# Where a float64 weight becomes two single-precision words: fewer steps on VectorE, and three GpSimd jobs moved to it

## The chip, the cores and the metric

The kernel runs on one core of a Trainium2 chip. Engines: TensorE (PE in the profile; PEld is its weight load), VectorE (DVE), ScalarE (ACT), GpSimd (POOL) and SyncE (SP), which only issues DMAs here. Each works through its own instruction list in order. The metric is the device time of one execution in microseconds (us).

## The reference

Three parts follow each other. All data are float32, except that `moe_w_in` and `moe_w_out` arrive as float64.

```python
# gated linear attention: q, k, v, f_logit are [4, 8, 768, 48]
f = 1 / (1 + exp(-f_logit))
for t in range(768):
    state = f[t] * state + outer(k[t], v[t]);  y[t] = q[t] @ state
x = y as [3072, 384]
# a dense FFN, w_in [384, 2048], w_out [2048, 384], both float64
h = x @ w_in
x = (max(h, 0) + log1p(exp(-|h|))) @ w_out
# a mixture of 8 experts on the tokens with x @ w_skip > 0
e = argmax(x @ w_gate);  p = softmax(x @ w_gate)[e]
out = x + p * (max(x @ w1[e], 0) @ w2[e])   # other tokens: out = x
```

## The kernel before

**Units and steps.** The FFN runs over 12 units of 256 tokens; each has 8 steps, one for each 256 columns of `w_in`. The main loop counts steps `s` from -20 to 95. A step of the FFN is `up` (matmuls of x with `w_in`), `act_a`, `act_b` and `act_c` (softplus) and `down` (matmuls with `w_out`). Every operand of these matmuls stands as two fp32r words, a rounded one (`hi`) and the remainder (`lo`), and three products are summed. Attention goes in 24 chunks of 128 tokens, in stages (`load`, `pre`, `decay`, `transpose`, `score`, `out`) that are laid some steps ahead of the unit that needs them. The experts follow behind unit 11.

**Conversion of the weights.** The float64 weights come in 8 groups (`load_w`): `si`, 256 columns of `w_in`, and `so`, 256 rows of `w_out`, 768 KB each, as pairs of 32-bit words. `conv_w(g, 0)` turns a group of `w_in` into `wi_hi`, `wi_lo`, and `conv_w(g, 1)` a group of `w_out` into `wo_hi`, `wo_lo`. The high word of a float64 holds its sign, an 11-bit exponent and 20 bits of the fraction; read as a float32 it is a float32 of another scale. The steps before: ScalarE takes the high word's absolute value (L218), VectorE clamps it from below (L220), masks and shifts it by 3 (L221), adds the two top bits of the high word (L222) and the top 3 bits of the low word (L223); ScalarE rounds the result to `hi` (L224), GpSimd subtracts to `lo` (L225). `tw` is the buffer that these steps share; there are two of it. For `so`, `route_cols` then multiplies the group with `w_skip` and `w_gate` on TensorE (L239 to L252). CONV_AT gives the step at which each group is converted: -8, -4, -1, 1, 2, 3, 4, 7. Groups 3 to 7 are so converted while unit 0 goes through its steps.

**Other work named below.** The gate's clamp (L273) is the first operation of `a_pre` on a chunk's `f_logit`, and waits for its DMA; the scans (L281, L282) of the same chunk read it, and free its buffer for the chunk two further on. For chunks 0 to 3 the clamp is VectorE's, from chunk 4 on GpSimd's (DVE_CHUNKS). In `act_c` the remainder `gl` (L442) is GpSimd's for the 8 steps of unit 0 (GL_POOL), and VectorE's from then on. GpSimd also has the addition of `act_b` (L433) and a mask for the first four chunks (L333).

**What sets the order.** The order in which the code issues instructions is only the start: a scheduler reorders each engine's list by a model of the times, except where the code pins it.

Of the kernel before, what the change touches and what calls it, by code (L numbers as in the profile page):

```python
# [40 lines left out]
def gla_softplus_moe_kernel(  # L41
# [156 lines left out]
    def load_w(g, parts=(0, 1)):
        n = 2 * P
        t = stage_t.setdefault(g, [None, None])  # L200
        if 0 in parts:
            t[0] = mw.tile([P, KD, 2 * n], I32, tag=f"w{2 * g % 4}", name=f"si{g}")
            sy.dma_start(out=t[0], in_=w_in32[:, g * 2 * n:(g + 1) * 2 * n].rearrange("(a p) c -> p a c", p=P))
        if 1 in parts:
            t[1] = mw.tile([P, 2, 2 * DM], I32, tag=f"w{2 * g % 4 + 1}", name=f"so{g}")
            sy.dma_start(out=t[1], in_=w_out32[g * n:(g + 1) * n, :].rearrange("(a p) c -> p a c", p=P))

    def conv_w(g, j):
        n = 2 * P
        src = stage_t[g][j].rearrange("p s (c two) -> p s c two", two=2)  # L210
# [5 lines left out]
        lo, hi = src[..., 0], src[..., 1]
        tf = t.bitcast(F32)
        se.activation(tf, hi.bitcast(F32), AF.Abs)  # L218

        (ge if 2 * g + j in MAX_POOL else ve).tensor_scalar(tf, tf, 2.0 ** -15, None, op0=ALU.max)  # L220
        ve.tensor_scalar(t, t, 0x07FFFFFF, 3, op0=ALU.bitwise_and, op1=ALU.logical_shift_left)  # L221
        ve.scalar_tensor_tensor(t, hi, -0x40000000, t, op0=ALU.bitwise_and, op1=ALU.bitwise_or)  # L222
# [952 lines left out]
```

## Time and profile before

| What | us |
|---|---|
| Median of 3 runs | 774.39 (773.63 to 779.21) |
| The profiled execution | 777.29 |
| Its span | 775.6 |
| TensorE busy (matmuls) | 703.9 |
| VectorE busy | 554.2 |
| ScalarE busy | 476.7 |
| GpSimd busy | 271.6 |

The span is the profiled execution's own, from its first to its last instruction. Busy time of an engine says little about a kernel of several stages: a table of stretches shows which engine is full in which stage, and the waits which engine the others wait for. A row's duration includes time in which the instruction could not get on.

### The profile page before, as it was taken

What the parts mean: (1) busy time and instruction counts of PE and PEld (TensorE: products, weight loads), DVE (VectorE), ACT (ScalarE), POOL (GpSimd) and SP (SyncE); (2) the same over time, 40 slices, a digit from 0 to 9 for tenths busy, and PEclk for the clock granted to TensorE, in tenths of its full rate; (3) what the DMA queues carried; (4) which work ended last, traced back from release to release, by engine and by line L of the source; (5) the groups of instructions that cost most, each with busy time, mean ns of one, the idle gap of its engine ahead of it and who ended that gap; (6) DMA issues with size and microseconds to landing.
All of it is one profiled execution on the core that took longest, in us unless ns stands there. A gap on an engine that the chain in (4) does not pass through costs nothing. (4 is left out here: it accounts for less than half of the span.)

```text
span 775.6 us, 15090 instructions
## 1 busy us (share of the span) xinstructions
PE 703.9 (91%) x5869; PEld 653.2 (84%) x5869; DVE 554.2 (71%) x1054; ACT 476.7 (61%) x863; POOL 271.6 (35%) x214
## 2 busy tenths in 40 slices
PE   2668788999999999999999999999989979999993
PEld 1557577898999999999999999999979878898883
DVE  8988997786767777767767786655866664865851
ACT  5647656566667667776666666755667643645750
POOL 4345775343343233423343232323322303321211
PEclk9869969799999999999999999999998999999997
DMA  9944421130213122211213122010423611655810
GB/s 293 258 149 129 128 83 43 53 95 25 72 53 95 53 75 69 59 54 48 89 53 96 53 63 62 14 46 8 159 67 121 252 42 51 209 204 179 292 74 11
DMA packets 36977, 77.19 MB, mean 100 GB/s; under 512 B 5967, under 2 KB 18594, under 8 KB 36896
## 3 DMA queue, kind: packets, MB, share of 16 engines
q1 hardware_dynamic: 34528, 71.89, 29.2%
q0 software_dynamic: 2368, 4.25, 1.9%
q8 instruction: 48, 0.79, 0.4%
q14 instruction: 33, 0.27, 0.1%
HBM read 64.89 MB, written 12.11 MB: 99 GB/s over the span
## 5 line engine op out<-in xcount | busy, mean ns | idle before, releaser
L406 PE MATMUL ph<-xh,wi 128*128 128x256 f32 x1152 | 235.6, 294 | 6.9 <-ACT wi L224 3.0
L433 POOL TENSOR_TENSOR w<-w,u 128x512 f32<-128x512 f32 x95 | 126.5, 1331 | 270.8 <-DVE u L426 182.0
L406 PEld LDWEIGHTS ph<-xh,wi 128*128 128x128 f32 x1152 | 193.1, 198 | 12.4 <-ACT wi L224 3.6
L406 PE MATMUL ph<-xl,wi 128*128 128x256 f32 x576 | 167.3, 290 | 0.6 <-DVE xl L383 0.6
L453 PE MATMUL acc<-wo_hi,gh 128*128 128x394 f32 x384 | 138.4, 362 | 3.0 <-ACT gh L441 2.4
L453 PE MATMUL acc<-wo_hi,gl 128*128 128x394 f32 x384 | 130.7, 348 | 3.8 <-DVE gl L442 3.4
L453 PE MATMUL acc<-wo_lo,gh 128*128 128x394 f32 x384 | 132.1, 344 | 0.0
L406 PEld LDWEIGHTS ph<-xl,wi 128*128 128x128 f32 x576 | 114.2, 198 | 1.3 <-DVE xl L383 0.9
L425 DVE SCALAR_TENSOR_TENSOR u<-w,u 128x512 f32<-128x512 f32 (+1 forms) x97 | 70.8, 731 | 37.2 <-ACT w L423 36.8
L442 DVE TENSOR_TENSOR gl<-w,gh 128x512 fp32r<-128x512 f32 (+1 forms) x89 | 60.9, 685 | 47.8 <-ACT gh L441 46.7
L421 ACT ACTIVATE u<-ph 128x512 f32<-128x512 f32 (+1 forms) x97 | 56.9, 587 | 49.8 <-PE ph L406 48.1
L432 ACT ACTIVATE w<-w 128x512 f32<-128x512 f32 (+1 forms) x97 | 60.7, 627 | 39.6 <-DVE u L425 39.5
L453 PEld LDWEIGHTS acc<-wo_hi,gh 128*128 128x128 f32 x384 | 72.8, 190 | 8.3 <-ACT gh L441 3.1
L441 ACT CAST gh<-w 128x512 fp32r<-128x512 f32 (+1 forms) x97 | 59.2, 611 | 30.8 <-POOL w L433 27.0
L453 PEld LDWEIGHTS acc<-wo_hi,gl 128*128 128x128 f32 x384 | 72.9, 190 | 5.9 <-DVE gl L442 4.5
L453 PEld LDWEIGHTS acc<-wo_lo,gh 128*128 128x128 f32 x384 | 73.6, 192 | 0.2 <-issue 0.2
L426 DVE SCALAR_TENSOR_TENSOR u<-ph,u 128x512 f32<-128x512 f32 (+1 forms) x97 | 65.8, 679 | 2.9
L651 DVE TENSOR_TENSOR w<-w,w 128x768 fp32r<-128x768 f32 x64 | 60.1, 984 | 8.1 <-ACT w L650 5.3
L423 ACT ACTIVATE w<-u 128x512 f32<-128x512 f32 (+1 forms) x97 | 60.6, 625 | 2.4 <-DVE gl L442 1.1
L422 ACT ACTIVATE u<-u 128x512 f32<-128x512 f32 (+1 forms) x97 | 60.7, 627 | 1.6
L766 PE MATMUL pom<-w,gh 128*128 128x384 f32 x208 | 55.8, 350 | 2.5 <-DVE om L776 2.5
L650 ACT CAST w<-w 128x768 fp32r<-128x768 f32 x64 | 49.7, 837 | 2.5 <-DMA w<-in_moe_w_dram 2.4
(197 smaller groups left out, 1233.3 us busy)
## 6 DMA issues: line engine op xcount, KB each, us to landing
w<-in_moe_w_dram SPq DMA_DIRECT2D x32, 768.0 KB
si<-in_moe_w_in_dram SPq DMA_DIRECT2D x8, 768.0 KB
so<-in_moe_w_out_dram SPq DMA_DIRECT2D x8, 768.0 KB
f<-in_f_logit_dram SPq DMA_DIRECT2D x24, 227.5 KB
q<-in_q_dram SPq DMA_DIRECT2D x24, 224.0 KB
k<-in_k_dram SPq DMA_DIRECT2D x24, 224.0 KB
x_s<-xr SPq DMA_DIRECT2D x24, 192.5 KB
v<-in_v_dram SPq DMA_DIRECT2D x24, 192.0 KB
```

The costliest lines, as they stand in the source:

```text
L406: te.matmul(ph[:, j, :], lhsT=w[i][:, kk, j * P:(j + 1) * P], rhs=x[:, kk, :], start=(n == 0), stop=(n == 3 * KD - 1))
L421: se.activation(u[:, c], ph[:, c], AF.Abs)
L422: se.activation(u[:, c], u[:, c], AF.Exp, scale=-1.0)
L423: se.activation(w[:, c], u[:, c], AF.Identity, bias=1.0)
L425: ve.scalar_tensor_tensor(u[:, c], w[:, c], 1.0, u[:, c], op0=ALU.subtract, op1=ALU.subtract)
L426: ve.scalar_tensor_tensor(u[:, c], ph[:, c], 0.0, u[:, c], op0=ALU.max, op1=ALU.subtract)
L432: se.activation(w[:, c], w[:, c], AF.Ln)
L433: (ve if i in self.fine else ge).tensor_tensor(w[:, c], w[:, c], u[:, c], op=ALU.add)
L441: se.copy(flat(gh)[:, c], w[:, c])
L442: (ge if i < self.pool_steps else ve).tensor_tensor(flat(gl)[:, c], w[:, c], flat(gh)[:, c].bitcast(F32), op=ALU.subtract)
L453: te.matmul(self.acc[t][:, 0:XR], lhsT=g[:, j, t * P:(t + 1) * P], rhs=w[f // 4][:, f % 4, :], start=(f == 0 and n == 0), stop=(f == NF - ...
L651: pin(ve.tensor_tensor(lo, t, hi.bitcast(F32), op=ALU.subtract))
```

## The change

ScalarE's pass takes the absolute value and scales it by 2**-112 at once, which puts the exponent where a float32 has it. The clamp (L220) is gone and the shift (L221) needs no mask; only the sign is taken from the high word. Three jobs of GpSimd go to VectorE: the weights' remainders (L225), the clamps of chunks 4 to 23 (L273), and unit 0's remainders `gl` (L442). The two weight tables are laid out anew before the launch, so that a group lies in one run of 6,144 bytes for each partition (before: three runs of 2,048 for `si`, two of 3,072 for `so`).

```diff
-DVE_CHUNKS = 4
-GL_POOL = 8
-MAX_POOL = ()
     def load_w(g, parts=(0, 1)):
...
+        for j in parts:
+            t[j] = mw.tile([P, 4 * DM], I32, tag=f"w{2 * g % 4 + j}", name=("si", "so")[j] + str(g))
+            sy.dma_start(out=t[j], in_=(w_in, w_out)[j][g].bitcast(I32))
     def conv_w(g, j):
...
-        se.activation(tf, hi.bitcast(F32), AF.Abs)
-        (ge if 2 * g + j in MAX_POOL else ve).tensor_scalar(tf, tf, 2.0 ** -15, None, op0=ALU.max)
-        ve.tensor_scalar(t, t, 0x07FFFFFF, 3, op0=ALU.bitwise_and, op1=ALU.logical_shift_left)
-        ve.scalar_tensor_tensor(t, hi, -0x40000000, t, op0=ALU.bitwise_and, op1=ALU.bitwise_or)
+        se.activation(tf, hi.bitcast(F32), AF.Abs, scale=2.0 ** -112)
+        ve.tensor_scalar(t, t, 3, None, op0=ALU.logical_shift_left)
+        ve.scalar_tensor_tensor(t, hi, -0x80000000, t, op0=ALU.bitwise_and, op1=ALU.bitwise_or)
         ve.scalar_tensor_tensor(t, lo, 29, t, op0=ALU.logical_shift_right, op1=ALU.bitwise_or)
-        se.copy(hw, tf)
-        ge.tensor_tensor(lw, tf, hw.bitcast(F32), op=ALU.subtract)
+        se.copy(hw, src)
+        ve.tensor_tensor(lw, src, hw.bitcast(F32), op=ALU.subtract)
     def a_pre(c):
-        (ge if c >= DVE_CHUNKS else ve).tensor_scalar(f, f, LOGIT_MIN, None, op0=ALU.max)
+        ve.tensor_scalar(f, f, LOGIT_MIN, None, op0=ALU.max)
     def act_c(self, i):
-                (ge if i < self.pool_steps else ve).tensor_tensor(flat(gl)[:, c], w[:, c], flat(gh)[:, c].bitcast(F32), op=ALU.subtract)
+                ve.tensor_tensor(flat(gl)[:, c], w[:, c], flat(gh)[:, c].bitcast(F32), op=ALU.subtract)
```

In the changed kernel's own line numbers L218 is L211, L221 to L225 are L212 to L216, L273 is L264, the scans L281 and L282 are L272 and L273, L300 is L291, L333 is L324, L433 is L423 and L442 is L432.

VectorE's list, from the first conversion step of group 0 on, before (`tw` is the conversion's buffer, `si` and `so` the loaded words, `qT`, `kT` and `f` attention's):

```order
L220 TENSOR_SCALAR tw<-tw 128x768
L221 TENSOR_SCALAR tw<-tw 128x768
L300 TENSOR_TENSOR qT_212<-q_130,eq_211 112x2x4x64
L222 SCALAR_TENSOR_TENSOR tw<-si_128,tw 128x768
L300 TENSOR_TENSOR kT_216<-k_132,ek_215 112x2x4x64
L223 SCALAR_TENSOR_TENSOR tw<-si_128,tw 128x768
L220 TENSOR_SCALAR tw<-tw 128x768
L273 TENSOR_SCALAR f_140<-f_140 112x520
L221 TENSOR_SCALAR tw<-tw 128x768
L222 SCALAR_TENSOR_TENSOR tw<-so_134,tw 128x768
L223 SCALAR_TENSOR_TENSOR tw<-so_134,tw 128x768
```

And now:

```order
L212 TENSOR_SCALAR tw<-tw 128x768
L213 SCALAR_TENSOR_TENSOR tw<-si_128,tw 128x768
L291 TENSOR_TENSOR qT_212<-q_130,eq_211 112x2x4x64
L291 TENSOR_TENSOR kT_216<-k_132,ek_215 112x2x4x64
L214 SCALAR_TENSOR_TENSOR tw<-si_128,tw 128x768
L212 TENSOR_SCALAR tw<-tw 128x768
L264 TENSOR_SCALAR f_140<-f_140 112x520
L213 SCALAR_TENSOR_TENSOR tw<-so_134,tw 128x768
L216 TENSOR_TENSOR wi_107<-tw,wi_107 128x768
L214 SCALAR_TENSOR_TENSOR tw<-so_134,tw 128x768
```

The two maxima (L220) are gone, and the first remainder (L216) stands between two steps of the next half's conversion.

GpSimd's list, behind its set-up, before:

```order
L225 TENSOR_TENSOR wi_107<-tw,wi_107 128x768
L333 AFFINE_SELECT a_sb<-a_sb 128x4x128
L225 TENSOR_TENSOR wo_lo_116<-tw,wo_hi_115 128x2x384
L333 AFFINE_SELECT a_sb<-a_sb 128x4x128
L225 TENSOR_TENSOR wi_108<-tw,wi_108 128x768
L225 TENSOR_TENSOR wo_lo_116<-tw,wo_hi_115 128x2x384
L273 TENSOR_SCALAR f_332<-f_332 112x520
L333 AFFINE_SELECT a_sb<-a_sb 128x4x128 x2
L273 TENSOR_SCALAR f_500<-f_500 112x520
L225 TENSOR_TENSOR wi_109<-tw,wi_109 128x768
L225 TENSOR_TENSOR wo_lo_118<-tw,wo_hi_117 128x2x384
```

And now:

```order
L324 AFFINE_SELECT a_sb<-a_sb 128x4x128 x6
L423 TENSOR_TENSOR w<-w,u 128x512 x3
L324 AFFINE_SELECT a_sb<-a_sb 128x4x128
L423 TENSOR_TENSOR w<-w,u 128x512
L324 AFFINE_SELECT a_sb<-a_sb 128x4x128
L423 TENSOR_TENSOR w<-w,u 128x512 x7
```

Of these only the masks (L333, now L324) and the additions (L433, now L423) stay on it.

VectorE's list from the scans of chunk 4 on (`f_332` before, `f_330` now), before:

```order
L281 SCALAR_TENSOR_TENSOR d_873<-restart,f_332 112x260
L282 SCALAR_TENSOR_TENSOR d_873<-restart,f_332 112x260
L252 TENSOR_TENSOR wo_lo_116<-pw_266,wo_hi_115 128x4x10
L222 SCALAR_TENSOR_TENSOR tw<-si_415,tw 128x768
L284 TENSOR_SCALAR hs_876<-d_873 112x4
L285 COPY hs_876<-d_873 112x4
L223 SCALAR_TENSOR_TENSOR tw<-si_415,tw 128x768
L315 TENSOR_TENSOR r_1035<-hs_587,hs_876 112x4
L286 TENSOR_TENSOR hmax<-hmax,hs_876 112x8
```

And now:

```order
L272 SCALAR_TENSOR_TENSOR d_862<-restart,f_330 112x260
L273 SCALAR_TENSOR_TENSOR d_862<-restart,f_330 112x260
L214 SCALAR_TENSOR_TENSOR tw<-si_411,tw 128x768
L216 TENSOR_TENSOR wo_lo_118<-tw,wo_hi_117 128x2x384
L309 TENSOR_TENSOR z_486<-ut,r_483 112x384
L243 TENSOR_TENSOR wo_lo_116<-pw_264,wo_hi_115 128x4x10
L275 TENSOR_SCALAR hs_865<-d_862 112x4
L276 COPY hs_865<-d_862 112x4
L216 TENSOR_TENSOR wi_110<-tw,wi_110 128x768
L264 TENSOR_SCALAR f_870<-f_870 112x520
```

Two remainders (L216) and the clamp of chunk 6 (L264, `f_870`) have come in; that clamp stands eight rows behind the scan which frees its buffer.

## Rows read from the trace of the kernel before

**Rows 1.** The profile's page: span and number of instructions.

```profile
span 775.6 us, 15090 instructions
```

**Rows 2.** Stretches: length, busy us of PE, PEld, DVE, ACT, POOL, PEclk, DMA, GB/s.

```profile
8.00:132.00 124.00, 91.00 (x765) 76.56 (x769) 112.63 (x155) 75.81 (x138) 70.64 (x42) 0.85 0.49 150
...
160.00:590.00 430.00, 424.75 (x3899) 401.93 (x3899) 302.91 (x651) 285.55 (x529) 147.77 (x114) 0.99 0.21 62
```

**Rows 3.** TensorE's waits, 8 to 132 us: us in total, times, longest.

```profile
PE pwt L239 <- DVE tw L223: 8.6, 4, 3.1
PE pw L244 <- DMA wsg<-in_moe_w_gate_dram: 4.5, 1, 4.5
```

**Rows 4.** VectorE's groups, 8 to 132 us: busy us, mean ns, idle before.

```profile
L221 DVE TENSOR_SCALAR tw<-tw 128x768 int32<-128x768 int32 x16 | 15.0, 938 | 0.2
L222 DVE SCALAR_TENSOR_TENSOR tw<-so,tw 128x768 int32<-128x768 int32 x8 | 11.6, 1448 | 0.1
L220 DVE TENSOR_SCALAR tw<-tw 128x768 f32<-128x768 f32 x16 | 11.6, 722 | 6.5 <-ACT tw L218 6.5
L222 DVE SCALAR_TENSOR_TENSOR tw<-si,tw 128x768 int32<-128x768 int32 x8 | 9.9, 1241 | 0.0
...
L284 DVE TENSOR_SCALAR hs<-d 112x4 f32<-112x4 f32 x6 | 5.5, 913 | 0.0
```

**Rows 5.** Instructions on the tile tw: shortest, median, longest in ns.

```profile
L220 DVE TENSOR_SCALAR tw<-tw x16: 528/553/1671, 8.0 to 127.3; 128x768 f32<-128x768 f32 x16
L221 DVE TENSOR_SCALAR tw<-tw x16: 546/556/3539, 8.5 to 128.0; 128x768 int32<-128x768 int32 x16
...
L224 ACT CAST wi<-tw x8: 817/832/835, 12.1 to 121.8; 128x768 fp32r<-128x768 f32 x8
```

**Rows 6.** The timeline, at 7 and around 42 us: start, duration, instruction.

```profile
7.21 0.14 DVE L284 TENSOR_SCALAR hs<-d 112x4 f32<-112x4 f32 x1
...
41.63 2.14 POOL L273 TENSOR_SCALAR f<-f 112x520 f32<-112x520 f32 x1
...
42.44 3.54 DVE L221 TENSOR_SCALAR tw<-tw 128x768 int32<-128x768 int32 x1
...
43.74 1.82 POOL L225 TENSOR_TENSOR wi<-tw,wi 128x768 fp32r<-128x768 f32 x1
```

**Rows 7.** Prices on VectorE: shortest, median, longest of three lines, whole run.

```profile
L651 DVE TENSOR_TENSOR w<-w,w x64: 945/952/2231, 574.4 to 749.9; 128x768 fp32r<-128x768 f32 x64
...
L442 DVE TENSOR_TENSOR gl<-w,gh x89: 418/685/873, 156.6 to 633.1; 128x512 fp32r<-128x512 f32 x87, 128x256 fp32r<-128x256 f32 x2
...
L273 DVE TENSOR_SCALAR f<-f x4: 422/426/851, 3.7 to 30.7; 112x520 f32<-112x520 f32 x4
```

**Rows 8.** GpSimd's groups, 8 to 132 us.

```profile
L225 POOL TENSOR_TENSOR wi<-tw,wi 128x768 fp32r<-128x768 f32 x8 | 15.8, 1977 | 17.3 <-ACT wi L224 17.3
L225 POOL TENSOR_TENSOR wo_lo<-tw,wo_hi 128x768 fp32r<-128x768 f32 x7 | 15.8, 2257 | 15.3 <-ACT wo_hi L224 15.3
L442 POOL TENSOR_TENSOR gl<-w,gh 128x512 fp32r<-128x512 f32 x7 | 12.6, 1799 | 3.0 <-ACT gh L441 3.0
L433 POOL TENSOR_TENSOR w<-w,u 128x512 f32<-128x512 f32 x7 | 9.9, 1409 | 7.2 <-DVE u L426 6.4 <-ACT w L432 0.8
L273 POOL TENSOR_SCALAR f<-f 112x520 f32<-112x520 f32 x5 | 9.5, 1907 | 6.8 <-DMA f<-in_f_logit_dram 6.8
L333 POOL TENSOR_SCALAR_AFFINE_SELECT a_sb<-a_sb 128x512 f32<-128x512 f32 x8 | 7.7, 983 | 3.1 <-ACT a_sb L332 3.0
```

**Rows 9.** The timeline: a gate's load and its clamp; a held-up conversion step.

```profile
54.30 0.33 SPq L263 DMA_DIRECT2D f<-in_f_logit_dram  x1
...
57.16 1.50 POOL L273 TENSOR_SCALAR f<-f 112x520 f32<-112x520 f32 x1 [5.59 <-DMA f<-in_f_logit_dram]
...
126.37 0.92 ACT L218 ACTIVATE tw<-so 128x768 f32<-128x768 f32 x1 [1.16 <-POOL wi L225]
...
127.32 0.67 DVE L220 TENSOR_SCALAR tw<-tw 128x768 f32<-128x768 f32 x1 [4.96 <-ACT tw L218]
```

More of the change, by code (lines that the diff above doesn't have):

```diff
@@ L47, in gla_softplus_moe_kernel @@
     f_logit: bass.AP,
-    w_in64: bass.AP,
-    w_out64: bass.AP,
+    w_in: bass.AP,
+    w_out: bass.AP,
     w_skip: bass.AP,
@@ L62, in gla_softplus_moe_kernel @@
     B = NT // S
-    DFF = w_in64.shape[1]
+    DFF = w_in.shape[0] * 2 * P
     E = w1.shape[0]
@@ L191, in clear_routes @@
         sy.dma_start(out=table.rearrange("(p c) o -> p (c o)", p=P), in_=t[:, 0:E * KT])
-    w_in32 = w_in64.bitcast(I32)
-    w_out32 = w_out64.bitcast(I32)
     stage_t = {}
     def load_w(g, parts=(0, 1)):
-        n = 2 * P
         t = stage_t.setdefault(g, [None, None])
[L201 to L206, printed above, removed]
+        for j in parts:
+            t[j] = mw.tile([P, 4 * DM], I32, tag=f"w{2 * g % 4 + j}", name=("si", "so")[j] + str(g))
+            sy.dma_start(out=t[j], in_=(w_in, w_out)[j][g].bitcast(I32))
@@ L208, in conv_w @@
     def conv_w(g, j):
-        n = 2 * P
-        src = stage_t[g][j].rearrange("p s (c two) -> p s c two", two=2)
-        t = att.tile([P, 2 * DM], I32, tag="tw", name="tw", bufs=2).rearrange("p (a c) -> p a c", a=src.shape[1])
+        lo, hi = (stage_t[g][j][:, n::2] for n in range(2))
+        t = att.tile([P, 2 * DM], I32, tag="tw", name="tw", bufs=2)
+        tf = t.bitcast(F32)
         if j == 0:
-            hw, lw = wi_hi[g], wi_lo[g]
+            hw, lw = (w[g].rearrange("p a c -> p (a c)") for w in (wi_hi, wi_lo))
+            src = tf
@@ L214, in conv_w @@
         else:
             hw, lw = (w[g // 2][:, g % 2 * 2:g % 2 * 2 + 2, 0:DM] for w in (wo_hi, wo_lo))
[L216 to L222 removed]
+            src = tf.rearrange("p (a c) -> p a c", a=2)
@@ L226, in conv_w @@
         if j == 1:
-            route_cols(g, tf)
+            route_cols(g, src)
     wt_ps = {}
@@ L391, in gla_softplus_moe_kernel, with __init__ @@
     class Ffn:
-        def __init__(self, x, fine=(), pool_steps=0):
+        def __init__(self, x, fine=()):
             self.x = x
             self.fine = fine
-            self.pool_steps = pool_steps
             self.h, self.w, self.cc, self.g = {}, {}, {}, {}
@@ L870, in gla_softplus_moe_kernel @@
                 if i == 0:
-                    ffns[u] = Ffn(xhl[u], FINE if u == NU - 1 else (), GL_POOL if u == 0 else 0)
+                    ffns[u] = Ffn(xhl[u], FINE if u == NU - 1 else ())
                 ffns[u].up(i)
@@ L1146, in _layout @@
         r = a.reshape(4, 2, -1, a.shape[1])
-        return _np.concatenate([r[:, :, :32].reshape(-1, a.shape[1]),
-                                r[:, :, 32:].transpose(0, 2, 1, 3).reshape(-1, a.shape[1])], 0)
+        r = _np.concatenate([r[:, :, :32].reshape(-1, a.shape[1]),
+                             r[:, :, 32:].transpose(0, 2, 1, 3).reshape(-1, a.shape[1])], 0)
+        return r.reshape(-1, P, a.shape[1] // 256, 256).transpose(2, 1, 0, 3).reshape(-1, P, 2 * r.shape[0])
+    if name == "moe_w_out":
+        return a.reshape(-1, 2, P, a.shape[1]).transpose(0, 2, 1, 3).reshape(-1, P, 2 * a.shape[1])
     return a
```

## The prediction

> **What bounds the kernel now.** I began with the span and the table of stretches [rows 1, 2]. From 160 to 590 us TensorE is busy for 424.75 of 430 us: nothing that VectorE (DVE), ScalarE (ACT) or GpSimd (POOL) saves there can shorten the run. The stretch to look at is 8 to 132 us, in which the eight groups of FFN weights are converted: VectorE is busy for 112.63 of 124 us, TensorE for 91.00, ScalarE for 75.81, GpSimd for 70.64 [rows 2]. TensorE's waits there end on VectorE's last conversion step (L223) for 8.6 us, and once on a DMA for 4.5 us [rows 3]. So VectorE sets the pace of this stretch, and 33 us of TensorE's idle time can be won at most.
>
> Next I looked at how VectorE spends its 112.63 us. Its rows are longer than their work. L221 averages 938 ns, with a median of 556; 16 of them are 15.0 - 16 x 0.556 = 6.1 us too long. L220 in the same way: 11.6 - 16 x 0.553 = 2.8. L222 against 0.952, the median of another two-input operation of its shape: 11.6 + 9.9 - 16 x 0.952 = 6.3 [rows 4, 5, 7]. L284 works on 4 columns; six of them take 5.5 us, where an undisturbed one takes 0.14: 4.7 [rows 4, 6]. The same reckoning for L223, L425, L281, L282, L300, L288, L315 and L318, each against its shortest row in the first 150 us, gives 13.1. Together 33 us. Where it comes from shows in one place: the L221 that starts at 42.44 us takes 3.54 us, and beside it GpSimd runs a gate clamp and then a remainder until 45.56 [rows 6]; VectorE ends 0.42 us after that. Of the 41 VectorE rows before 145 us that are stretched by over 0.1 us, all overlap a GpSimd instruction. So VectorE pays for work that stands on GpSimd's list.
>
> **The change part by part.** All of it falls into the same stretch, but for 15 later clamps.
>
> The max on VectorE (L220) goes: 16 x 0.553 = -8.8 us [rows 5]. The step after it keeps its shape and loses one of two operations; a one-operation L220 and a two-operation L221 on the same shape take 0.553 and 0.556 [rows 5], so that is nothing. ScalarE's pass keeps its count and shape: a scale in it costs nothing that I can price, and ScalarE has 48 us free here [rows 2].
>
> The remainders of the split (L225) go to VectorE: 16 instructions. The same shape, types and operation stands on VectorE at L651 with a median of 952 ns [rows 7]: +15.2. Unit 0's eight remainders (L442), of which GpSimd ran seven in this stretch [rows 8]: 7 x 0.685 [rows 7] = +4.8. The clamps (L273), five here [rows 8]: 5 x 0.424 (four of them ran on VectorE, shortest 422 ns [rows 7]) = +2.1. Work on VectorE: -8.8 + 15.2 + 4.8 + 2.1 = +13.3.
>
> Against that the stretching. GpSimd's time here is 15.8 + 15.8 + 12.6 + 9.5 = 53.7 us in what moves away, and 9.9 + 7.7 = 17.6 in what stays (L433, L333) [rows 8]. Shared out by time, 75% of the 33 us go: -24.8. The bounds: at best all 33 go; at worst what stays stretches a denser VectorE by all of its 17.6 us in place of 8.2, and only 33 - 17.6 = 15.4 go. I take the share, since the pairs of rows give about the same (L225 alone some 15.6 us of the stretch).
>
> The Trainium skill (SBUF — State Buffer, section "Who interferes with whom") says that VectorE and GpSimd share one pair of ports, and that who comes first holds it for the whole instruction while the other is blocked; that agrees with the 3.54 us row. By this rule alone, with every microsecond of the moved work blocking, 53.7 us would go and the run would gain some 40 us; the measured stretch of 33 us in all refuses that.
>
> A hold-up goes too. At 127.32 us VectorE had been idle for 4.96 us for ScalarE's next pass, and that pass had waited for GpSimd to finish a remainder, since it writes the buffer the remainder reads [rows 9]; before that the GpSimd queue held up an addition as well. With remainders of 0.95 us in place of about 2 us [rows 7, 8], I take 4 of the 4.96: -4.0 (bounds 0 and -4.96).
>
> New waits. VectorE takes its list in order, so each moved instruction can now stop it. (a) A remainder needs ScalarE's cast, 0.832 us [rows 5]. In the new order the work between a group's L223 and its remainder is 1.4 us at the least and mostly 2 to 4, so 0. (b) A clamp needs its gate's DMA, which is issued only when the scan two chunks earlier has freed the buffer. At 54.30 us that load is issued and at 57.16 the clamp starts, 2.9 us later, after 5.59 us of GpSimd's idling [rows 9]. The new order puts 3.0 to 4.2 us of other VectorE work between scan and clamp for chunks 5 to 8, so a prompt load is hidden; SyncE's queue is in order too, and may not be prompt. Bounds 0 and 5.6 each; I take 0.7 each for five, the nearer row being the 2.9 against 3.0: +3.5. (c) Up to 30 us the load engines are full, and TensorE waits 4.5 us for the small gate weights [rows 3]; a faster VectorE then reaches work that TensorE has not finished. Bounds 0 and 6; I take +3.0.
>
> The weight tables are laid out anew, so that each of a partition's loads is one run of 6 KB in place of three of 2 or two of 3. No row prices that; the bytes stay, and I take nothing, with 1 us either way. From 160 to 590 us VectorE has 127 us free [rows 2], which covers 15 clamps of 0.42 us and the last remainder of unit 0.
>
> Sum for VectorE's stretch: +13.3 - 24.8 - 4.0 + 3.5 + 3.0 = -9.0 us. TensorE follows it, since its idle time here (33 us) is well above that. The profiled execution took 777.29 us (span 775.6 us [rows 1] and 1.7 us around it); it would take 768.3. It lies 2.9 above the median of 774.39, so the forecast is **765.4 us**, 1.2% below. With the bounds above, the gain is between 0 and about 18: the forecast's own range is 757 to 772.
>
> **The rivals.**
>
> *TensorE is the next bound.* It is busy for 91.00 of the 124 us [rows 2]. If half of VectorE's saving lands where TensorE is full, the gain is 4.5 us: 770. Against it: the waits on VectorE's steps stand at the top of its list [rows 3].
>
> *The clock gives more.* The granted clock was 0.85 in 8 to 132 us and 0.99 in 160 to 590 [rows 2]: in the stretch with the gaps TensorE is at the lower of its two levels (1.2 in place of 2.4 GHz) for some three tenths of the time. At full clock the same work would have taken about 91.00 x 0.15 = 14 us less. If a denser TensorE wins 8 of these where it is itself the bound, the time is 757. It is as likely that the lower level just falls elsewhere, so I leave this out of the sum.
>
> *VectorE stands behind late gates (slower).* If each of the five clamps waits as GpSimd's did at 57.16, 5.6 us [rows 9], that is 28 us in place of 3.5: -9.0 + 24.5 = +15.5, so 790. It decides from 2.5 us a clamp: there the gain is gone. The order speaks against it (3.0 us of cover at the least), the single SyncE queue for it.
>
> *VectorE only gets more work (slower).* If the stretch is VectorE's own and stays, +13.3 - 4.0 + 6.5 = +15.8: 790. The overlap of all 41 stretched rows with GpSimd speaks against it. The Trainium skill (Perfetto Trace Analysis, section "Optimizing Scalar/DVE Operations") says that a saturated VectorE may give work to GpSimd, which this change undoes; it adds at once that between these two that may not help.
>
> **How the numbers follow.** The forecast gets 0.52, TensorE as the bound 0.26, the clock 0.11, late gates 0.07, more work 0.04. A difference of 1%, 7.7 us, is about what a measurement of this kernel tells from no change (its three runs spread over 5.6 us); faster by over 1% means under 766.6. Of the forecast's 0.52 some 0.43 lie below that, with all of the clock's 0.11: 0.54 faster. The rest of the forecast and all of the second case give 0.35 within 1%. The two slower ones give 0.11. The range has to reach the second case and the clock's: 756 to 776; left out are the two slower cases and the tails.
>
> **What would show it.** In 8 to about 122 us of the changed profile: no max; 16 remainders on VectorE of about 0.95 us; GpSimd busy for under 20 us; the last conversion step near 122 us in place of 132; L221's mean near 0.6 us, and L284's near 0.2. TensorE busy without a gap from then on. Wrong would be: VectorE rows still stretched where GpSimd is idle (the stretch was VectorE's own); VectorE idle for more than 12 us in the stretch, ended by the gate's DMA or by ScalarE's casts (the new waits were too small); the last conversion step at 122 us but the run no shorter, with the time back as TensorE's idle time behind 132 us or as a lower granted clock.

## The result, and the profile after

The changed kernel takes 754.84 us (median of four runs, 753.31 to 757.98), the kernel before beside it 775.92 us (773.63 to 779.21). The ratio is 0.973, with a 95% interval of 0.968 to 0.978: 21 us or 2.7% faster. I had forecast 765.4 us, 9 us below before, with a range that began at 756.

The profiled execution of the changed kernel took 757.98 us, its longest, against 777.29 us for the one of before. From its page: the span, and each engine's busy time with its share and instructions.

```profile
span 756.3 us, 15057 instructions
...
PE 695.6 (92%) x5869; PEld 644.7 (85%) x5869; DVE 539.2 (71%) x1082; ACT 476.1 (63%) x863; POOL 198.5 (26%) x170
```

VectorE's and GpSimd's busy times have both fallen, by 15 and 73 us; ScalarE's has stayed (against the table of the time before). Where they fell, the table of stretches shows (length, busy us of PE, PEld, DVE, ACT, POOL, then PEclk, DMA share, GB/s). The last conversion step now ends at 112.54 us in place of 132.16, so the first row here answers to the 8 to 132 us of before [rows 2].

```profile
8.00:114.00 106.00, 84.57 (x792) 70.31 (x794) 98.76 (x168) 75.82 (x138) 23.77 (x15) 0.94 0.54 175
...
160.00:590.00 430.00, 424.84 (x3863) 402.69 (x3862) 299.10 (x652) 283.42 (x523) 125.56 (x99) 0.99 0.23 70
```

In 106 us VectorE is busy for 98.76 (93%), GpSimd for 23.77 where it had 70.64, and TensorE for 84.57 at a granted clock of 0.94 (before: 0.85). From 160 to 590 us nothing has changed, as one expects of a stretch that TensorE fills. VectorE's groups in 8 to 114 us (busy us, mean ns, idle before):

```profile
L212 DVE TENSOR_SCALAR tw<-tw 128x768 int32<-128x768 int32 x16 | 9.8, 610 | 2.3 <-ACT tw L211 2.3
L213 DVE SCALAR_TENSOR_TENSOR tw<-so,tw 128x768 int32<-128x768 int32 x8 | 8.7, 1090 | 0.1
L216 DVE TENSOR_TENSOR wo_lo<-tw,wo_hi 128x768 fp32r<-128x768 f32 x8 | 8.5, 1068 | 0.4 <-ACT wo_hi L215 0.3
L213 DVE SCALAR_TENSOR_TENSOR tw<-si,tw 128x768 int32<-128x768 int32 x8 | 7.6, 951 | 0.0
L216 DVE TENSOR_TENSOR wi<-tw,wi 128x768 fp32r<-128x768 f32 x8 | 7.6, 950 | 0.0
...
L432 DVE TENSOR_TENSOR gl<-w,gh 128x512 fp32r<-128x512 f32 x7 | 4.8, 682 | 2.4 <-ACT gh L431 2.4
...
L264 DVE TENSOR_SCALAR f<-f 112x520 f32<-112x520 f32 x8 | 3.8, 470 | 1.8 <-DMA f<-in_f_logit_dram 1.8
...
L275 DVE TENSOR_SCALAR hs<-d 112x4 f32<-112x4 f32 x6 | 2.5, 410 | 0.0
```

Line by line against [rows 4]: the max is gone, the shift (L212, was L221) takes 610 ns in place of 938, the step after it 951 and 1090 in place of 1241 and 1448, the four columns of L275 410 in place of 913. The 16 remainders (L216) have come in at 950 and 1068 ns. VectorE's waits there (us in total, times, longest):

```profile
DVE gl L432 <- ACT gh L431: 2.4, 1, 2.4
DVE tw L212 <- ACT tw L211: 2.3, 5, 0.6
DVE f L264 <- DMA f<-in_f_logit_dram: 1.8, 1, 1.8
```

And TensorE's:

```profile
PE pk L299 <- DVE kT L291: 10.9, 1, 10.9
...
PE pw L235 <- DMA wsg<-in_moe_w_gate_dram: 4.5, 1, 4.5
...
PE pwt L230 <- DVE tw L214: 1.5, 2, 1.2
```

TensorE waits for the last conversion step for 1.5 us, where it was 8.6 [rows 3]; the wait for the small gate weights is the same 4.5. The first line is the start-up, TensorE's wait for the first `kT`; before it was 11.3 us, the longest of TensorE's waits there, which [rows 3] doesn't show. Its last 3 us come after the 8 us mark, so they are among the 33 us of idle time that the prediction counted as there to be won. What is left on GpSimd in the same stretch:

```profile
L423 POOL TENSOR_TENSOR w<-w,u 128x512 f32<-128x512 f32 x7 | 12.7, 1814 | 31.5 <-DVE u L416 20.1 <-ACT w L422 6.3 <-ACT w L413 5.2
L324 POOL TENSOR_SCALAR_AFFINE_SELECT a_sb<-a_sb 128x512 f32<-128x512 f32 x8 | 11.2, 1403 | 47.6 <-ACT a_sb L323 47.6
```

Both groups have grown longer, the addition from 1409 to 1814 ns and the mask from 983 to 1403 [rows 8]. TensorE's wait for a mask is 1.6 us (before: 2.3), so that costs little. That the denser VectorE does it is not shown: in e6 below VectorE is as full (94% of the stretch), and the mask takes 922 ns.

The end of FFN unit 0 shows that the whole gain arises here: the timeline's copy of its first result (start, duration, instruction) in the kernel before,

```profile
155.74 0.49 ACT L473 COPY xr<-acc 128x394 f32<-128x394 f32 x1 [0.50 <-PE acc L453]
```

and in the changed one:

```profile
133.32 0.47 ACT L463 COPY xr<-acc 128x394 f32<-128x394 f32 x1
```

That is 22.4 us earlier. The eleven units behind it end 40 to 48 us apart in both kernels and give back 3 us in all; the span is 19.3 us shorter.

**One account for every kernel.** I take the stretch from VectorE's first conversion step (7.96 us) to the end of the last one, and split its length in three: *idle* is the sum of the waits that the timeline gives behind VectorE's rows; *stretching* is the sum over its rows of what each takes beyond the shortest row of its line and shape in the first 150 us; *work* is the rest. In us, of the profiled executions, one for each kernel; GpSimd's busy time and the granted clock are those of the stretch, and "unit 0" is the start of the copy above.

| kernel | time, median | ratio to before, 95% | stretch | work | stretching | idle | GpSimd busy | clock | unit 0 |
|---|---|---|---|---|---|---|---|---|---|
| before | 775.92 | | 124.2 | 79.5 | 34.0 | 10.7 | 70.6 | 0.85 | 155.7 |
| changed | 754.84 | 0.9730 (0.9679 to 0.9782) | 104.6 | 90.1 | 8.0 | 6.5 | 23.8 | 0.93 | 133.3 |
| e1_moves | 762.28 | 0.9803 (0.9761 to 0.9845) | 111.0 | 97.1 | 8.7 | 5.2 | 25.0 | 0.95 | 138.6 |
| e2_nomax | 768.86 | 0.9894 (0.9859 to 0.9929) | 120.3 | 72.0 | 28.2 | 20.1 | 72.8 | 0.86 | 150.1 |
| e3_layout | 774.12 | 0.9974 (0.9945 to 1.0003) | 127.7 | 79.5 | 34.5 | 13.7 | 70.8 | 0.91 | 158.5 |
| e4_ghost | 764.64 | 0.9848 (0.9806 to 0.9889) | 115.4 | 88.7 | 16.9 | 9.8 | 83.9 | 0.87 | 143.8 |
| e5_rest_back | 760.59 | 0.9795 (0.9766 to 0.9824) | 110.2 | 84.1 | 15.1 | 11.1 | 41.5 | 0.83 | 139.9 |
| e6_split_back | 764.26 | 0.9841 (0.9816 to 0.9866) | 111.8 | 77.1 | 29.3 | 5.4 | 49.7 | 0.85 | 143.2 |
| e7_masks | 748.65 | 0.9651 (0.9630 to 0.9671) | 105.1 | 94.6 | 7.3 | 3.2 | 12.1 | 0.97 | 130.7 |
| e8_hold | 765.67 | 0.9878 (0.9850 to 0.9905) | 120.2 | 90.8 | 23.9 | 5.5 | 90.3 | 0.86 | 146.8 |
| e9_adds | 748.83 | 0.9648 (0.9601 to 0.9695) | 97.1 | 92.7 | 3.5 | 0.9 | 10.5 | 0.93 | 128.9 |
| e10_masks_adds | 754.59 | 0.9726 (0.9677 to 0.9774) | 101.2 | 96.7 | 1.7 | 2.8 | 0.0 | 0.93 | 135.1 |
| e11_masks_only | 766.37 | 0.9887 (0.9859 to 0.9916) | 118.3 | 84.5 | 28.3 | 5.6 | 67.7 | 0.88 | 142.4 |
| e12_warm | 754.80 | 0.9723 (0.9684 to 0.9761) | 102.6 | 89.7 | 8.4 | 4.6 | 25.7 | 0.98 | 132.3 |

So the change made VectorE's stretch 19.6 us shorter: +10.6 of work, -26.0 of stretching, -4.2 of idling.

### The profile page after: what moved, and what is told of

Same layout as the page of the kernel before. It is cut to its first block, busy times and chain, and to the rows that moved or that the text cites. A ratio compares the mean times of both kernels' runs of the same rounds, so it can differ in the third digit from the quotient of the medians.

```text
span 756.3 us, 15057 instructions
## 1 busy us (share of the span) xinstructions
PE 695.6 (92%) x5869; PEld 644.7 (85%) x5869; DVE 539.2 (71%) x1082; ACT 476.1 (63%) x863; POOL 198.5 (26%) x170
## 5 line engine op out<-in xcount | busy, mean ns | idle before, releaser
L396 PE MATMUL ph<-xh,wi 128*128 128x256 f32 x1152 | 230.8, 289 | 2.0 <-DVE wi L216 1.0
L423 POOL TENSOR_TENSOR w<-w,u 128x512 f32<-128x512 f32 x95 | 128.7, 1355 | 339.2 <-DVE u L416 213.4
L396 PEld LDWEIGHTS ph<-xh,wi 128*128 128x128 f32 x1152 | 188.9, 194 | 7.0 <-issue 2.4
L396 PE MATMUL ph<-xl,wi 128*128 128x256 f32 x576 | 164.5, 286 | 0.0
L396 PEld LDWEIGHTS ph<-xl,wi 128*128 128x128 f32 x576 | 111.9, 194 | 0.0
L432 DVE TENSOR_TENSOR gl<-w,gh 128x512 fp32r<-128x512 f32 (+1 forms) x97 | 65.9, 681 | 46.2 <-ACT gh L431 45.5
L415 DVE SCALAR_TENSOR_TENSOR u<-w,u 128x512 f32<-128x512 f32 (+1 forms) x97 | 67.8, 699 | 34.1 <-ACT w L413 33.8
L411 ACT ACTIVATE u<-ph 128x512 f32<-128x512 f32 (+1 forms) x97 | 57.2, 589 | 51.6 <-PE ph L396 49.8
```

The costliest lines, as they stand in the source:

```text
L396: te.matmul(ph[:, j, :], lhsT=w[i][:, kk, j * P:(j + 1) * P], rhs=x[:, kk, :], start=(n == 0), stop=(n == 3 * KD - 1))
L411: se.activation(u[:, c], ph[:, c], AF.Abs)
L415: ve.scalar_tensor_tensor(u[:, c], w[:, c], 1.0, u[:, c], op0=ALU.subtract, op1=ALU.subtract)
L423: (ve if i in self.fine else ge).tensor_tensor(w[:, c], w[:, c], u[:, c], op=ALU.add)
L432: ve.tensor_tensor(flat(gl)[:, c], w[:, c], flat(gh)[:, c].bitcast(F32), op=ALU.subtract)
```

## Experiments

My theory: VectorE sets the pace of the conversion; its rows are stretched by what GpSimd does beside them, and work that leaves GpSimd takes the stretching along. The rivals: the gain comes from the max alone, or from the new layout of the weights; TensorE's clock gives it; GpSimd's remainders cost by holding the buffer `tw`, and not by slowing VectorE's rows.

### The three parts of the change, each alone

**e1_moves**: before, with the three moved jobs on VectorE; max, masks and layout stay.

```diff
-DVE_CHUNKS = 4
+DVE_CHUNKS = 24
-GL_POOL = 8
+GL_POOL = 0
-        ge.tensor_tensor(lw, tf, hw.bitcast(F32), op=ALU.subtract)
+        ve.tensor_tensor(lw, tf, hw.bitcast(F32), op=ALU.subtract)
```

> The kernel before with only the three jobs moved to VectorE: the max, the mask and the old layout stay. My theory (VectorE is stretched by GpSimd's work, and sets the pace of the stretch): +22 us of work, -25 us of stretching and -4 us of hold-up, so 4 to 13 us faster than before, with GpSimd busy under 25 us up to the last conversion step and VectorE's L284 near its undisturbed 0.14 us. Rival 1 (the removed max alone makes the gain, a job costs the same on either engine): within 3 us of before, or slower. Rival 2 (the stretching is VectorE's own): 15 us or more slower.

Measured: 762.28 us against 776.86 of before beside it, -14.6 us. Stretching falls from 34.0 to 8.7 us, work grows by 17.6, idling halves. The 14.6 us are 1.6 more than the expectation's range allowed. By the prediction's own terms the moves were worth next to nothing: -24.8 + 15.2 + 4.8 + 2.1 - 4.0 + 6.5 = -0.2 us. Here lies the whole miss. The account puts the stretch at -13.2 us, 13.0 from that sum: the waits came 8.0 us lower (-5.5 for +2.5), the work 4.5 lower (17.6 for 22.1) and the stretching 0.5.

**e2_nomax**: before, with the new arithmetic alone.

```diff
-        se.activation(tf, hi.bitcast(F32), AF.Abs)
-        (ge if 2 * g + j in MAX_POOL else ve).tensor_scalar(tf, tf, 2.0 ** -15, None, op0=ALU.max)
-        ve.tensor_scalar(t, t, 0x07FFFFFF, 3, op0=ALU.bitwise_and, op1=ALU.logical_shift_left)
-        ve.scalar_tensor_tensor(t, hi, -0x40000000, t, op0=ALU.bitwise_and, op1=ALU.bitwise_or)
+        se.activation(tf, hi.bitcast(F32), AF.Abs, scale=2.0 ** -112)
+        ve.tensor_scalar(t, t, 3, None, op0=ALU.logical_shift_left)
+        ve.scalar_tensor_tensor(t, hi, -0x80000000, t, op0=ALU.bitwise_and, op1=ALU.bitwise_or)
```

> The kernel before with only the new arithmetic: scale in ScalarE's pass, no max, no mask; the three jobs stay on GpSimd, the old layout stays. My theory: VectorE saves 16 x 0.55 = 8.8 us and is stretched as before, so 7 to 12 us faster. Rival 1 (the max alone makes the gain): 18 to 22 us faster. A third reading, that the collisions just move to other rows and take the saving back: within 3 us of before.

Measured: 768.86 against 776.86, -8.0 us, close to the -8.8 that the prediction gave the max. The account shows that it is not that simple: work and stretching fall by 13.3 us together, and 9.4 come back as idling. VectorE's waits in 8 to 128 us:

```profile
DVE tw L220 <- ACT tw L218: 13.2, 5, 6.4
```

ScalarE's pass writes a buffer that GpSimd's remainder reads, so the hold-up of [rows 9] is the first suspect; e8 below puts it to the test. In the longest wait, the 6.4 us up to 123.85, ScalarE's list stood behind GpSimd three times: 1.60 us for a clamp, 0.97 for an addition and 1.15 for the buffer.

**e3_layout**: before, with the new layout of the weights alone (in the changed kernel the old arithmetic, and the three jobs on GpSimd again).

```diff
-        se.activation(tf, hi.bitcast(F32), AF.Abs, scale=2.0 ** -112)
-        ve.tensor_scalar(t, t, 3, None, op0=ALU.logical_shift_left)
+        se.activation(tf, hi.bitcast(F32), AF.Abs)
+        ve.tensor_scalar(tf, tf, 2.0 ** -15, None, op0=ALU.max)
+        ve.tensor_scalar(t, t, 0x07FFFFFF, 3, op0=ALU.bitwise_and, op1=ALU.logical_shift_left)
...
-        ve.tensor_tensor(lw, src, hw.bitcast(F32), op=ALU.subtract)
+        ge.tensor_tensor(lw, src, hw.bitcast(F32), op=ALU.subtract)
```

> The kernel before with only the new layout of the two weight tables, one run of 6144 bytes a partition. My theory: within 3 us of before. Rival 3 (fuller loads in the first 30 us start everything sooner): 5 us or more faster, with TensorE's wait for the small gate weights shorter than 4.5 us.

Measured: 774.12 against 776.86; the interval of the ratio, 0.9945 to 1.0003, holds 1. The layout is worth nothing that this measurement can tell. The parts add up: -14.6 and -8.0 make -22.6, the change gave -21.1. In the profiled executions the stretch is 13.2 and 3.9 us shorter and 3.5 us longer than before in e1, e2 and e3, and their times lie at -14.4, -4.4 and +1.6; the first two make 17.1 of the 19.6 us by which the change shortens it, so there the sum holds only roughly. Neither the max alone nor the layout carries the gain.

### Does GpSimd's reading alone slow VectorE?

**e4_ghost**: the changed kernel, with four reads by GpSimd beside each conversion; they touch no buffer that VectorE waits for, and their result is not used.

```diff
         ve.tensor_tensor(lw, src, hw.bitcast(F32), op=ALU.subtract)
+        gt = att.tile([P, P + 64], F32, tag="gt", name="gt", bufs=1)
+        for n in range(4):
+            part = hw[:, n * 192:(n + 1) * 192] if j == 0 else hw[:, n // 2, n % 2 * 192:(n % 2 + 1) * 192]
+            ge.tensor_tensor(gt, part.bitcast(F32), part.bitcast(F32), op=ALU.subtract)
```

> The changed kernel, in which GpSimd also reads each new hi word again and writes a difference that nobody uses: 64 instructions of 128x192, no buffer of the conversion is held by them. My theory: GpSimd's reads alone stretch VectorE again, 10 to 18 us slower than the changed kernel, VectorE's rows longer where they overlap L220 on GpSimd. Rival 2 (the stretching is VectorE's own, GpSimd's time is free): within 3 us of the changed kernel. They also stand ahead of the masks and additions in GpSimd's list, which may add a few us in either theory.

Measured: 764.64 us, some 9.8 above the changed kernel (ratios 0.985 and 0.973), where 10 to 18 were expected. Stretching goes from 8.0 to 16.9. GpSimd's added groups in 8 to 123 us:

```profile
L220 POOL TENSOR_TENSOR gt<-wi 128x192 f32<-128x192 f32 x32 | 36.7, 1147 | 12.6 <-ACT wi L215 10.6
L220 POOL TENSOR_TENSOR gt<-wo_hi 128x192 f32<-128x192 f32 x28 | 23.3, 831 | 13.6 <-ACT wo_hi L215 12.1
```

So work on GpSimd that nobody waits for lengthens VectorE's rows, at a low price: 60 us of these reads add 8.9 us of stretching. The run's 9.8 us are not that alone. The reads stand in GpSimd's list ahead of masks and additions; TensorE waits 8.1 us for late masks (changed kernel: 1.6), and VectorE once 4.1 us for TensorE:

```profile
PE py L350 <- POOL a_sb L328: 8.1, 3, 5.3
```

In e8, next, the masks are hardly late, and the stretching stands by itself.

**e8_hold**: e4 with one of the two inputs taken from the buffer `tw`, so that GpSimd holds it as the old remainder did.

```diff
-            ge.tensor_tensor(gt, part.bitcast(F32), part.bitcast(F32), op=ALU.subtract)
+            full = src[:, n * 192:(n + 1) * 192] if j == 0 else src[:, n // 2, n % 2 * 192:(n % 2 + 1) * 192]
+            ge.tensor_tensor(gt, full, part.bitcast(F32), op=ALU.subtract)
```

> The changed kernel with the same idle readers on GpSimd as in the run with the unused differences, but their first operand is now the conversion buffer, so that it is held until GpSimd is done. My theory: GpSimd's busy time and the stretching as in that run, VectorE's idle time in the stretch up by 6 us or more, so 4 to 10 us slower than that run. Rival (the hold-up is hidden): within 2 us of that run.

Measured: 765.67 us, ratio 0.9878 (0.9850 to 0.9905) against 0.9848 (0.9806 to 0.9889) of e4. VectorE idles for 5.5 us, less than in e4 (9.8), and TensorE's wait for masks is down to 1.8. Other waits in 8 to 128 us:

```profile
ACT tw L211 <- POOL gt L221: 9.2, 8, 2.3
...
DVE tw L212 <- ACT tw L211: 1.8, 4, 0.7
```

ScalarE's pass waits 9.2 us for the held buffer, but VectorE waits for that pass only 1.8 us (changed kernel: 2.3). So the hold-up reaches ScalarE and not VectorE, and the 4 to 10 us expected over e4 did not come; the 13.2 us of e2 don't come of it alone. The rest of e2's idling I leave open: its order of work is another one too. Against the changed kernel e8 has 15.9 us more of stretching, 0.7 more of work and 1.0 less of idling; the conversion ends 15.6 us later, and the run takes 10.8 us more. This is the plainest case of GpSimd's work lengthening VectorE's rows, and the run with them.

### Which of the moved jobs counts

**e5_rest_back**: the changed kernel with the clamps of chunks 4 and up and unit 0's remainders on GpSimd again.

```diff
-        ve.tensor_scalar(f, f, LOGIT_MIN, None, op0=ALU.max)
+        (ge if c >= 4 else ve).tensor_scalar(f, f, LOGIT_MIN, None, op0=ALU.max)
...
-                ve.tensor_tensor(flat(gl)[:, c], w[:, c], flat(gh)[:, c].bitcast(F32), op=ALU.subtract)
+                (ge if i < self.pool_steps else ve).tensor_tensor(flat(gl)[:, c], w[:, c], flat(gh)[:, c].bitcast(F32), op=ALU.subtract)
```

(`pool_steps` is 8 for unit 0, else 0.)

> The changed kernel with the clamps and unit 0's remainders given back to GpSimd; the weights' remainders stay on VectorE. My theory now (the stretch of VectorE's conversion is its own work, plus GpSimd's busy time as stretching, plus idle time while a remainder on GpSimd holds the conversion buffer): 7 us less work, 10 to 12 us more stretching, no more idle time, so 2 to 6 us slower than the changed kernel. Rival (all three jobs cost the same by GpSimd's time, no buffer is held up): 8 us slower, 22 of the 54 us of GpSimd's moved time.

**e6_split_back**: the changed kernel with the remainders of the weights' split on GpSimd again.

```diff
-        ve.tensor_tensor(lw, src, hw.bitcast(F32), op=ALU.subtract)
+        ge.tensor_tensor(lw, src, hw.bitcast(F32), op=ALU.subtract)
```

> The changed kernel with the weights' remainders alone given back to GpSimd. My theory now: 15 us less work on VectorE, 14 to 18 us more stretching, and 8 to 13 us more idle time before the first conversion step, as ScalarE's next pass waits for the buffer: 8 to 14 us slower than the changed kernel. Rival (no buffer is held up): the work and the stretching cancel, within 3 us.

Measured: 760.59 and 764.26 us, 5.8 and 9.4 above the changed kernel. Together 15.2; both put back at once (e2, with the layout that counts nothing) give 14.0. The jobs add up. Both totals lie in the ranges expected, but not by the parts: e5 has 7.1 us more of stretching (10 to 12 expected) and 4.6 more of idling (none expected); e6 has 21.3 more of stretching (14 to 18) and 1.1 less of idling, where 8 to 13 more were expected. Those totals were right by luck. In e6 GpSimd's remainders in 8 to 120 us,

```profile
L216 POOL TENSOR_TENSOR wi<-tw,wi 128x768 fp32r<-128x768 f32 x8 | 18.6, 2325 | 22.0 <-ACT wi L215 22.0
L216 POOL TENSOR_TENSOR wo_lo<-tw,wo_hi 128x768 fp32r<-128x768 f32 x7 | 13.1, 1866 | 27.7 <-ACT wo_hi L215 27.7
```

and what they do to VectorE rows of quite another kind, which take 765, 470 and 682 ns in the changed kernel:

```profile
L272 DVE TENSOR_TENSOR_SCAN d<-restart,f 112x260 f32<-112x260 f32 x6 | 7.8, 1308 | 0.0
...
L264 DVE TENSOR_SCALAR f<-f 112x520 f32<-112x520 f32 x8 | 7.4, 920 | 0.9 <-DMA f<-in_f_logit_dram 0.9
L432 DVE TENSOR_TENSOR gl<-w,gh 128x512 fp32r<-128x512 f32 x6 | 6.8, 1136 | 0.0
```

What a microsecond of GpSimd costs VectorE in stretching is not one number. Against the changed kernel: e6 +25.9 us of GpSimd, +21.3 of stretching (0.82); e5 +17.7 and +7.1 (0.40); e4 +60.1 and +8.9 (0.15); e8 +66.5 and +15.9 (0.24).

### Is it the clock?

**e12_warm**: the changed kernel with 72 matmuls of 128 x 256 more, twelve behind each of the first six halves, into a PSUM bank that is free; nothing uses them.

```diff
+        if g < 3:
+            warm = ps.tile([P, 512], F32, tag="acc1", name="warm")
+            col = hw if j == 0 else hw[:, 0]
+            for n in range(12):
+                te.matmul(warm[:, 0:256], lhsT=col[:, 0:P], rhs=col[:, 0:256], start=(n == 0), stop=(n == 11))
```

> The changed kernel with 72 extra matmuls (128x256, results not used) on the first six converted halves, into a PSUM bank that is still free: they fill TensorE's gaps up to some 50 us. Reading that the granted clock made part of the gain: the clock from 30 to 60 us goes from 0.78 to over 0.9, and unit 0's end comes 2 us or more sooner. My theory (VectorE sets the pace up to the last conversion step): the clock rises, the last conversion step and unit 0's end stay within 2 us or come later by what the extra matmuls take; 0 to 6 us slower.

The stretch from 30 to 60 us of the changed kernel (the third number from the end is the granted clock):

```profile
30.00:60.00 30.00, 24.81 (x258) 20.16 (x257) 27.56 (x51) 20.77 (x40) 6.37 (x5) 0.78 0.56 179
```

and of e12:

```profile
30.00:60.00 30.00, 26.14 (x313) 22.20 (x310) 29.65 (x54) 25.14 (x48) 7.91 (x5) 1.00 0.63 194
```

The clock rises from 0.78 to 1.00, the conversion ends 2.0 us earlier, unit 0 1.0 us earlier, and the run takes 754.80 us, as against 754.84. The added matmuls take time of TensorE's own, so a small gain may hide behind them; of the 8 us that the rival asked for nothing is seen. In this stretch of the changed kernel a higher clock buys nothing that can be measured. No run raises the clock in the kernel before.

### Going on: the rest of GpSimd's work

**e7_masks**: the changed kernel, with the masks of the first four chunks on VectorE as those of the later chunks are (VectorE's predicated copy in place of ScalarE's copy and GpSimd's mask).

```diff
-MASK_ACT = 4
+MASK_ACT = 0
```

> The changed kernel with the masks of the first four chunks on VectorE too, straight from PSUM as for the later chunks: 8 masks of about 1 us leave GpSimd, 8 copies leave ScalarE, 8 instructions of 0.73 us come to VectorE. My theory: +5.8 us of work, -3 to -4 of stretching, a shorter way from the scores to their product; within 3 us of the changed kernel, more likely slower. Rival (what is left of GpSimd costs most): 3 us or more faster.

**e9_adds**: the changed kernel, with unit 0's additions (L423) on VectorE.

```diff
-                (ve if i in self.fine else ge).tensor_tensor(w[:, c], w[:, c], u[:, c], op=ALU.add)
+                (ve if i in self.fine or self.early else ge).tensor_tensor(w[:, c], w[:, c], u[:, c], op=ALU.add)
```

(`early` is true for unit 0.)

> The changed kernel with unit 0's eight additions on VectorE as well. My theory (a GpSimd microsecond costs VectorE 0.3 to 0.6 of stretching): 7 x 0.69 = 4.8 us of work for 3 to 6 us of stretching, so within 3 us of the changed kernel; 3 us or more faster if the shorter way from the softplus to the down matmuls counts.

**e10_masks_adds**: both edits.

> Masks and unit 0's additions both on VectorE, so that GpSimd does nothing while weights are converted. If the two add up: the masks' 6 us and what the additions alone give. VectorE's L275 at its undisturbed 0.14 us and no stretched row up to the last conversion step. If VectorE's work is now the price: no better than with the masks alone (748.7).

**e11_masks_only**: before, with `MASK_ACT = 0`.

> The kernel before with only the masks of the first four chunks moved to VectorE. If the masks' gain comes from the shorter way from the scores to their product and from ScalarE's freed copies, it shows here too: 3 to 7 us faster than before. If it needs a VectorE that is not stretched: within 3 us of before, since 5.8 us of work replace 3 to 4 us of stretching.

Measured: e7 748.65 us and e9 748.83 us, each 6 us below the changed kernel and with no run in common with its range; the interval of e7's ratio lies clear of the changed kernel's, that of e9 overlaps it by 0.0016. Both together: 754.59, no gain. And on the kernel before the masks alone are worth 10 us (766.37 against 776.43), more than the 6 here. Of the expectations, e9's second one came (3 us or more faster, by the shorter way to the `down` matmuls). For e7 my theory said within 3 us and more likely slower. e10 had no stretched row up to the last conversion step, as expected, but is 6 us slower than the masks alone, and neither reading foresaw that. e11 lies beyond its 3 to 7 us.

In e9 GpSimd goes from 23.8 to 10.5 us, stretching from 8.0 to 3.5, idling from 6.5 to 0.9, and the conversion ends 7.5 us earlier. Work grows by 2.6, so stretching and work give 1.9 of the 7.5 us and the shorter waits 5.6. With the masks moved as well, VectorE has 4.0 us more work and 1.9 more idling, and 1.8 less of stretching: the conversion ends 4.1 us later than in e9. Behind it TensorE is nearly full. The stretches from about the end of the conversion to the end of unit 0, in e7, e9 and e10 (length, busy us of PE, PEld, DVE, ACT, POOL, clock, DMA share, GB/s):

```profile
113.00:131.00 18.00, 18.00 (x215) 15.79 (x214) 16.05 (x30) 13.88 (x28) 3.85 (x3) 1.00 0.35 105
```

```profile
105.00:129.00 24.00, 23.09 (x262) 20.13 (x263) 21.01 (x41) 16.19 (x33) 3.81 (x2) 1.00 0.37 100
```

```profile
109.00:118.00 9.00, 7.38 (x107) 5.95 (x106) 6.69 (x13) 6.44 (x12) 0.00 (x0) 1.00 0.30 89
118.00:127.00 9.00, 9.00 (x52) 7.61 (x52) 6.84 (x15) 2.80 (x7) 1.28 (x1) 0.62 0.18 53
127.00:136.00 9.00, 9.00 (x104) 8.44 (x96) 6.51 (x12) 6.85 (x14) 1.29 (x1) 1.00 0.37 103
```

TensorE is busy all or nearly all the time in all three, but for 109 to 118 us in e10 (7.38 of 9). In e10 it got 0.62 of its clock in 118 to 127 us, where e7 and e9 have 1.00: 9.0 x 0.38 = 3.4 us. With the 4.1 us that makes 7.5, more than enough for the 6.2 by which unit 0 ends later than in e9. This is read from one execution each and was not tried by an experiment. Where e7's 6 us come from is not shown. Its conversion ends no earlier (105.1 against 104.6 us) and its unit 0 2.7 us earlier; the other 6.6 of the 9.3 us between the two profiled executions lie behind unit 0, where the edit changes no instruction but the order can differ, and the changed kernel's profiled execution was its slowest.

## Why the prediction was right in kind and wrong in size

**What bounds the kernel: right.** VectorE's stretch became 19.6 us shorter, the span 19.3. e12 shows that TensorE's clock does not set the pace there, and e8 that lengthening VectorE's rows lengthens the run.

**Stretching: right, -26.0 us for -24.8.** The moved jobs took three quarters of it along. The share by time held in total only, and so far by luck: by job the price of a GpSimd microsecond ran from 0.15 to 0.82.

**Work: +10.6 us for +13.3.** I multiplied by durations. VectorE's rows overlap at their ends, and what counts is from start to start. The timeline of the changed kernel (start, duration, instruction):

```profile
12.31 0.95 DVE L213 SCALAR_TENSOR_TENSOR tw<-so,tw 128x768 int32<-128x768 int32 x1
13.18 0.95 DVE L216 TENSOR_TENSOR wi<-tw,wi 128x768 fp32r<-128x768 f32 x1
14.04 0.95 DVE L214 SCALAR_TENSOR_TENSOR tw<-so,tw 128x768 int32<-128x768 int32 x1
14.91 0.70 DVE L272 TENSOR_TENSOR_SCAN d<-restart,f 112x260 f32<-112x260 f32 x1
```

A row of 0.95 us is followed 0.87 us later. 15 remainders lie within the stretch (the last stands behind the last conversion step), and 15 x 0.87 + 7 x 0.61 + 5 x 0.34 = 19.0, less some 8 for the max by the same spacing: +11.

**The step that failed: the waits in "+13.3 - 24.8 - 4.0 + 3.5 + 3.0 = -9.0 us".** I had them at +2.5 in all; they measured -4.2, and term (c) made most of it.

- The hold-up of ScalarE's pass, -4.0: 6.5 us [rows 4] became 2.3. Right.
- (a) waits for casts, 0: the wait of L432 for its cast, 2.4 us once; none of the split's within the stretch.
- (b) clamps behind late loads, +3.5: one of five waited, and for 1.8 us.

```profile
50.01 0.43 DVE L264 TENSOR_SCALAR f<-f 112x520 f32<-112x520 f32 x1 [1.77 <-DMA f<-in_f_logit_dram]
```

- (c) waits for TensorE and the loads, +3.0: they went the other way, -4.2. The timeline of before has the wait, for TensorE's scores:

```profile
60.47 0.69 DVE L300 TENSOR_TENSOR kT<-k,ek 112x512 f32<-112x512 f32 x1 [3.76 <-PE pc L328]
```

  The changed kernel has none like it, nor the 0.4 us before an L425 (for ScalarE). I had only asked what a faster VectorE would run into, and not which waits of the old order would go. Why this one went is open. The moves are one candidate: e3, with the jobs on GpSimd, has the like (3.15 us at 59.82), e1 has none; but e2, with the jobs on GpSimd too, has none either. TensorE's clock is another. In before the scores stood behind matmuls that ran at the lower of TensorE's two levels:

```profile
50.00:58.00 8.00, 6.54 (x27) 5.76 (x28) 6.03 (x13) 4.00 (x10) 2.41 (x2) 0.50 0.63 186
```

  In e3 the clock was at 0.50 from 50.4 to 57.2 us too; in the changed kernel it was at 1.00 from 50 to 55. No run raises the clock in the kernel before, so this rival stands untested for that wait.

Term by term the 10.6 us between -9.0 and -19.6 are: (c) 7.2, work 2.7, (b) 1.7, stretching 1.2, the hold-up 0.2, and (a) 2.4 the other way. That attribution is bookkeeping on one execution of each kernel; e1 confirms its place (the moves, -14.6 us) and that the waits are its largest part (8.0 of 13.0 us), but not each term. Idling is no steady quantity either: with the same jobs on GpSimd it is 10.7, 13.7 and 20.1 us in before, e3 and e2.

**The rivals.** TensorE as the next bound (770): not yet here, its waits for L214 fell to 1.5 us, and it still has gaps behind the conversion (2 us for `xr`, 1.1 for a mask); it comes in e7 and e9, behind the conversion. The clock (757): the granted clock rose from 0.85 to 0.93; e12 shows that a further rise to 0.98 buys nothing, and not what the first one gave. Beside the wait above, from the end of the conversion to unit 0's end it may have given the 2.8 us by which that piece is shorter (20.8 us at 1.00, before 23.6 at 0.78); the later units gave back 3 us. Late gates (790): 1.8 us in place of 28. More work for VectorE (790): refused by the stretching, 34.0 to 8.0. Of the signs named, the shift's mean came (610 ns for 0.6 us). The last conversion step came at 112.5 us in place of 122, and TensorE was not without a gap from then on. GpSimd kept 23.8 us for under 20, and the four-column step took 410 ns for 200: VectorE stayed stretched by what was left on GpSimd.

The Trainium skill (Perfetto Trace Analysis, section "Optimizing Scalar/DVE Operations") says that a saturated VectorE may hand work to GpSimd, and that between these two it might not help. e1 is the measured case of the second half: three jobs, 17.6 us of work by the account, put back on a VectorE that was 91% busy [rows 2] saved 14.6 us.

**The range.** Its lower end does not follow from the bounds listed. At their best these give 13.3 - 33 - 4.96 = -24.7 us, which is 749.7 from the median of 774.39; the prediction said "about 18" without a sum, and set the range at 756. 754.84 lies just below the range, and within the bounds. The bounds of the waits were wrong besides: they ended at zero, where a wait could also vanish.

## What to carry to other kernels

If VectorE sets the pace and its rows are longer than the shortest of their kind, look for GpSimd work beside the long ones; moving that work onto VectorE can pay although VectorE is full, as long as there is stretching to win (here it paid from 34 us of stretching down to 8; the additions paid again, more by shorter waits, and with them moved the masks paid nothing). Price a moved instruction by the spacing of starts in a dense row of the trace, and ask of each wait in the old timeline whether the new order still has it. Put each half back by itself before believing a sum: the parts added up here, the price per microsecond did not carry over.
